# Counting eight rows of choices: one scan on VectorE and one product with ones instead of eight products

## The chip, the cores and the metric

The kernel runs on one core of a Trainium2 chip. The time is the device time of one execution in microseconds (us), as a median over several runs. The profile is of one further execution, taken by the hardware profiler. The engines are named as the profile names them: PE (TensorE, matrix products; PEld is its weight loads), DVE (VectorE), ACT (ScalarE), POOL (GpSimd), SP (SyncE, which here only issues transfers).

## The reference

A batch of 4 column-normalised attentions (over 5056 rows and 256 channels each) gives 20224 tokens of 256 channels; each token then goes to one of 8 experts, the one with the largest logit.

```python
qn = q / (norm(q, axis=1) + 1e-6);  kn = k / (norm(k, axis=1) + 1e-6)     # B, N, C = 4, 5056, 256
a = softmax(kn.T @ qn / tau)                                              # 256 x 256 for each batch
x = (v @ a).reshape(20224, 256)
logits = x @ w_gate;  e = argmax(logits)                                  # 8 experts
gate = softmax(logits)[e];  eom = sigmoid(x @ w_output_gate)[e]
out = gate * eom * (relu(x @ w1[e]) @ w2[e])                              # w1: 256 x 1024, w2: 1024 x 256
```

## The kernel before, in words

The program has three stages, which overlap.

1. `gram(b)`, one for each batch b: q and k are loaded in 20 steps of 256 rows (tiles `qk`, 6 buffers), PE adds `k.T @ q` into `s_ps` (line 467), ACT squares the same tile (line 428) and DVE adds the squares into `acc` (line 429). At the end the softmax of the 256 x 256 matrix is taken; `ah` and `al` are its high and low parts, with the attention's product with both gate matrices as 16 further columns.
2. `mix(b)`: the rows of v (tiles `v`, 4 buffers, 4 rows of each partition) are transposed on PE into `vt_ps` (line 582), split by ACT and DVE into `vh` and `vl`, and multiplied by `ah` and `al` into `x_ps` (lines 615 to 617, 272 columns: 256 of x, 8 logits, 8 output gates). ACT copies the result into `st` (line 618). A group is 128 partitions by R = 8 rows; a batch has 5 groups, the four batches 20.
3. After each group `route(b, g, st)` finds every token's expert, and a slot for it in that expert's region of the scratch `xs_d` in memory; POOL then scatters the group's 8 rows of tokens there by 8 indirect transfers (line 693). Later `blocks` fetches blocks of 256 or 128 tokens of one expert, with that expert's weights, and runs the two expert products (`h_ps`, lines 1038 to 1040; `y_ps`, lines 1063 to 1065), which take most of the time.

Stage 2 for batch b is interleaved with stage 1 for the next batches by the generator `_beside` and the rate `GRATE`. Within what the generators give, the framework's scheduler sets the order of instructions on each engine from the dependencies and its own model of durations. So a change of few instructions can move others.

In `route`, on DVE: `m` is the largest logit, `val` marks the experts that reach it, `mv` picks the first of them, and `oh` (line 656, in bfloat16, 128 x (8 rows x 8 experts)) is one where a token chose an expert. For a token in partition p and row t, its slot needs the number of earlier tokens of the group with the same choice: the tokens of the partitions above p in the same row count, and all tokens of the earlier rows (t' < t) count. PE gets this in `r_ps`, which has 9 rows of 8 columns: the product with the triangle `tri` (line 677) gives the first part, and eight products with the all-ones matrix `onesb` (line 680) add row t's total to all rows behind t; the ninth row is the total of the group. DVE then adds the running start `rco` (line 685), keeps the chosen column (line 686), sums it to the slot `si` (line 689), and moves `rco` on (line 690). The products of a group are issued one turn after its choices were found.

Of the kernel before, what the change touches and what calls it, by code (L numbers as in the profile page):

```python
# [10 lines left out]
BF16 = mybir.dt.bfloat16  # L11
F32 = mybir.dt.float32
# [3 lines left out]
ALU = mybir.AluOpType  # L16
# [4 lines left out]
P = 128  # L21
# [17 lines left out]
def tile_colnorm_attention_then_top1_moe(  # L39
# [12 lines left out]
    nc = tc.nc  # L52
    B, N, C = q.shape
    E = w_gate.shape[1]
# [6 lines left out]
    R = 8  # L61
# [32 lines left out]
    cst = ctx.enter_context(tc.tile_pool(name="cst", bufs=1))  # L94
# [4 lines left out]
    sm = ctx.enter_context(tc.tile_pool(name="sm", bufs=2))  # L99
# [49 lines left out]
    onesb = cst.tile([P, P], BF16, name="onesb")  # L149
# [3 lines left out]
        out=tri, in_=onesb, pattern=[[1, P]], compare_op=ALU.is_gt, fill=0.0, base=0, channel_multiplier=-1  # L153
# [10 lines left out]
    for b in range(B):  # L164
# [9 lines left out]
        out=real, in_=onesf[:, 0:1], pattern=[[0, 1]], compare_op=ALU.is_ge, fill=0.0, base=LASTP - 1,  # L174
# [6 lines left out]
        out=mine, in_=onesf[:, :E], pattern=[[-16, E]], compare_op=ALU.is_ge, fill=0.0, base=0, channel_multiplier=1  # L181
    )
    nc.gpsimd.affine_select(
        out=mine, in_=mine, pattern=[[16, E]], compare_op=ALU.is_ge, fill=0.0, base=15, channel_multiplier=-1
# [12 lines left out]
    nc.vector.memset(done, 0.0)  # L197
    invw = cst.tile([P, 2, E], F32, name="invw")
    nc.vector.memset(invw, 0.0)
    rank = cst.tile([P, E, E], F32, name="rank")  # L200
    rcr = cst.tile([P, E], F32, name="rcr")
    eor = cst.tile([P, E], F32, name="eor")
# [20 lines left out]
    def main(**ins):  # L223
        last.update((e, i.ins) for e, i in ins.items())

    @contextmanager
    def behind(*engines):
        with ExitStack() as held_back:
            for e in engines:
                if e in last:  # L230
                    held_back.enter_context(tc.issue_after(last[e]))
            yield
# [14 lines left out]
    def grouped(ins, group, why):  # L247
        tc.declare_no_dep(ins.ins, group=group, reason=why)
        tc.add_to_no_dep_group(group, ins.ins)
# [341 lines left out]
    def mix(b):  # L591
# [6 lines left out]
        for j in range(total):  # L598
            g, i = divmod(j, R // 2)
            n = b * total + j + AHD  # L600
            if n < B * total:
                turn(*divmod(n, total))
            if i == 0:
                if b == B - 1 and g == 1:
                    st = wide(f"st{b}_{g}")
                else:
                    st = wk.tile([P, R, CW], F32, tag="st", name=f"st{b}_{g}", bufs=STB)
                if b == B - 1 and g == 0:
                    sts["void"] = st
            vh, vl = turned.pop(0)  # L610
            for t in range(2):
                x_ps = ps_x.tile([P, 512], F32, tag="x", name="x_ps")
                for c in range(CC):
                    tsl = slice(t * P, (t + 1) * P)
                    nc.tensor.matmul(x_ps[:, :CW], vh[:, c, tsl], ah[:, c, :], start=c == 0, stop=False)  # L615
                    nc.tensor.matmul(x_ps[:, :CW], vh[:, c, tsl], al[:, c, :], start=False, stop=False)  # L616
                    ins = nc.tensor.matmul(x_ps[:, :CW], vl[:, c, tsl], ah[:, c, :], start=False, stop=c == CC - 1)  # L617
                main(PE=ins, ACT=nc.scalar.copy(st[:, 2 * i + t, :], x_ps[:, :CW]))  # L618
            if i == RLATE:
                finish(later)  # L620
            yield
            if i == R // 2 - 1:
                later = route(b, g, st)
                next(later)
# [5 lines left out]
    def route(b, g, st):  # L630
        lastg = g == NG - 1
        lg = st[:, :, C : C + E]
        og = st[:, :, C + E :]

        def t3(tag, dt=F32):
            return sm.tile([P, R, E], dt, tag=tag, name=tag)

        def t2(tag, dt=F32):
            return sm.tile([P, R], dt, tag=tag, name=tag)

        def bc(a):
            return a.unsqueeze(2).to_broadcast([P, R, E])

        def bce(a):
            return a.unsqueeze(1).to_broadcast([P, R, E])

        m = t2("r_m")
        nc.vector.tensor_reduce(out=m, in_=lg, axis=AX.X, op=ALU.max)
        d = t3("r_d")
        nc.vector.tensor_tensor(out=d, in0=lg, in1=bc(m), op=ALU.subtract)  # L650
        val = t3("r_val")
        nc.vector.scalar_tensor_tensor(out=val, in0=d, scalar=0.0, in1=bce(c8), op0=ALU.is_ge, op1=ALU.mult)
        mv = t2("r_mv")
        nc.vector.tensor_reduce(out=mv, in_=val, axis=AX.X, op=ALU.max)
        oh = t3("r_oh", BF16)
        nc.vector.tensor_tensor(out=oh, in0=val, in1=bc(mv), op=ALU.is_equal)
        if lastg and LASTP < P:
            nc.vector.tensor_scalar(out=oh, in0=oh, scalar1=real, scalar2=None, op0=ALU.mult)
        nc.scalar.activation(d, d, AF.Exp)
        se = t2("r_se")  # L660
        nc.vector.tensor_reduce(out=se, in_=d, axis=AX.X, op=ALU.add)
        nc.vector.tensor_scalar(out=se, in0=se, scalar1=1e-9, scalar2=None, op0=ALU.add)
        os_ = t3("r_os")
        nc.vector.tensor_tensor(out=os_, in0=og, in1=oh, op=ALU.mult)
        og1 = t2("r_og1")
        nc.vector.tensor_reduce(out=og1, in_=os_, axis=AX.X, op=ALU.add)
        nc.scalar.activation(og1, og1, AF.Exp, scale=-1.0)
        gt = t2("r_gt")
        nc.vector.scalar_tensor_tensor(out=gt, in0=og1, scalar=1.0, in1=se, op0=ALU.add, op1=ALU.mult)
        nc.vector.reciprocal(st[:, :, C + 1], gt)  # L670
        nc.scalar.copy(st[:, :, C].bitcast(I32), ids[:, b, g * R : (g + 1) * R])

        yield
        r_ps = ps_x.tile([P, 512], F32, tag="x", name="r_ps")
        rv = r_ps[:, : (R + 1) * E].rearrange("p (r e) -> p r e", e=E)
        with behind("PE"):
            nc.tensor.matmul(rv[:, :R, :], tri, oh, start=True, stop=False, skip_group_check=True)
            for t in range(R):
                n = R - t
                nc.tensor.matmul(  # L680
                    rv[:, t + 1 :, :], onesb, oh[:, t, :].unsqueeze(1).to_broadcast([P, n, E]),
                    start=False, stop=t == R - 1, skip_group_check=True,
                )
        rk = t3("r_rk")
        nc.vector.tensor_tensor(out=rk, in0=rv[:, :R, :], in1=bce(rco), op=ALU.add)
        nc.vector.tensor_tensor(out=rk, in0=rk, in1=oh, op=ALU.mult)
        si = sm.tile([P, R], I32, tag="r_si", name="r_si", bufs=6)
        with nc.allow_low_precision(reason="one of the terms is a whole number of a slot, the others are zero"):
            nc.vector.tensor_reduce(out=si, in_=rk, axis=AX.X, op=ALU.add)
        nc.vector.tensor_tensor(out=rco, in0=rv[:, R, :], in1=rco, op=ALU.add)  # L690
        for t in range(R):
            np_ = LASTP if lastg else P
            ins = nc.gpsimd.indirect_dma_start(  # L693
                out=xs_d[:, :],
                out_offset=bass.IndirectOffsetOnAxis(ap=si[:np_, t : t + 1], axis=0),
                in_=st[:np_, t, :].bitcast(I32),
                in_offset=None,
                bounds_check=NSLOT - 1,
                oob_is_err=False,
            )  # L700
            grouped(ins, "xs", "each token has a slot of its own; readers wait for a mark read after the scatters")
            main(POOL=ins)
# [501 lines left out]
```

## Time and profile before

| | |
|---|---|
| median of 3 runs (lowest to highest) | 1277.83 us (1277.14 to 1281.59) |
| the profiled execution: time, span | 1289.07 us, 1287.4 us |
| mean granted clock of PE, share of full speed | 0.967 |
| busy: PE, DVE, ACT, POOL | 1210.2, 705.6, 621.7, 572.3 us |
| products with `onesb` of `route` (line 680) | 160, of 64 down to 8 columns |
| products with `tri` (line 677) | 20, of 64 columns |

The busy time is the union of an engine's instructions, so overlapping ones count once. The profiled execution was 11.2 us longer than the median of the runs shown; durations below are from it.

### The profile page before, as it was taken

What the parts mean: (1) busy time and instruction counts of PE and PEld (TensorE: products, weight loads), DVE (VectorE), ACT (ScalarE), POOL (GpSimd) and SP (SyncE); (2) the same over time, 40 slices, a digit from 0 to 9 for tenths busy, and PEclk for the clock granted to TensorE, in tenths of its full rate; (3) what the DMA queues carried; (4) which work ended last, traced back from release to release, by engine and by line L of the source; (5) the groups of instructions that cost most, each with busy time, mean ns of one, the idle gap of its engine ahead of it and who ended that gap; (6) DMA issues with size and microseconds to landing.
All of it is one profiled execution on the core that took longest, in us unless ns stands there. A gap on an engine that the chain in (4) does not pass through costs nothing.

```text
span 1287.4 us, 27771 instructions
## 1 busy us (share of the span) xinstructions
PE 1210.2 (94%) x10412; PEld 1084.0 (84%) x10412; DVE 705.6 (55%) x2123; ACT 621.7 (48%) x1233; POOL 572.3 (44%) x561
## 2 busy tenths in 40 slices
PE   8999899997857999999999999999999899999998
PEld 7888788887755888888888888888888789999997
DVE  6668447544646765555565555544453355455552
ACT  5578448545542665455554555433333234344442
POOL 0004654654455224445544455544444454444443
PEclk9999899897878999999999999999999899999999
DMA  9976776754548787473646553843323633346743
GB/s 309 331 248 217 237 228 227 241 165 157 187 139 264 209 218 183 87 208 72 187 102 174 108 141 95 239 124 76 68 68 114 142 64 80 84 79 161 206 113 128
DMA packets 175170, 208.54 MB, mean 162 GB/s; under 512 B 120968, under 2 KB 124558, under 8 KB 170296
## 3 DMA queue, kind: packets, MB, share of 16 engines
q1 hardware_dynamic: 130600, 126.58, 35.1%
q0 software_dynamic: 43312, 79.73, 21.7%
q8 instruction: 84, 1.38, 0.5%
q14 instruction: 54, 0.44, 0.1%
q10 hardware_dynamic: 1120, 0.42, 0.1%
HBM read 275.55 MB, written 61.41 MB: 262 GB/s over the span
## 4 chain that ended last, share of the span: by engine, by line
PE 81%; issue 6%; DMA 4%; DVE 3%; POOL 2%; another core or an unknown queue 2%; ACT 1%; POOLq 0%; SPq 0%; DVEq 0%; ACTq 0%
PE h_ps L1040 10%; PE h_ps L1038 10%; PE h_ps L1039 10%; PE y_ps L1063 10%; PE y_ps L1065 10%; PE y_ps L1064 9%; PE s_ps L467 9%; PE x_ps L615 4%; PE x_ps L617 3%; PE x_ps L616 3%; PE vt_ps L582 3%; DMA qk<-in_k_dram 2%; POOL out_dram L1076 1%; DMA wbuf<-wsc,wi 1%
## 5 line engine op out<-in xcount | busy, mean ns | idle before, releaser
L1043 DVE SCALAR_TENSOR_TENSOR hb<-h_ps,hb 128x512 f16<-128x512 f32 (+1 forms) x360 | 226.7, 635 | 353.6 <-ACT hb L1042 265.1
L1038 PE MATMUL h_ps<-xt,wbuf 128*128 128x256 f16 (+1 forms) x1440 | 368.6, 264 | 7.3 <-DMA wbuf<-wsc,wi 4.2
L1040 PE MATMUL h_ps<-xt,wbuf 128*128 128x256 f16 (+1 forms) x1440 | 368.7, 264 | 5.2 <-issue 5.2
L1039 PE MATMUL h_ps<-xt,wbuf 128*128 128x256 f16 (+1 forms) x1440 | 368.7, 264 | 3.0 <-issue 2.8
L1065 PE MATMUL y_ps<-wbuf,hb 128*128 128x256 f16 x1296 | 354.1, 273 | 4.4 <-DVE tb_at L720 1.9
L1042 ACT ACTIVATE hb<-h_ps 128x512 f16<-128x512 f32 (+1 forms) x360 | 193.8, 550 | 340.0 <-PE h_ps L1040 238.5
L1063 PE MATMUL y_ps<-wbuf,hb 128*128 128x256 f16 x1296 | 354.5, 274 | 2.7 <-issue 2.6
L1064 PE MATMUL y_ps<-wbuf,hb 128*128 128x256 f16 x1296 | 354.4, 273 | 1.6 <-issue 1.5
L931 POOL DMA_INDIRECT wbuf<-wsc,wi x166 | 176.4, 1063 | 224.9 <-PE h_ps L1040 166.9
L693 POOL DMA_INDIRECT xs_d<-st,r_si x160 | 167.7, 1048 | 235.8 <-ACT st L618 139.4
L1076 POOL DMA_INDIRECT out_dram<-yo,b_id x162 | 171.3, 1057 | 85.7 <-issue 43.2
L1038 PEld LDWEIGHTS <-wbuf 128*128 128x128 f16 x1440 | 141.9, 99 | 22.6 <-DMA wbuf<-wsc,wi 4.5
L1040 PEld LDWEIGHTS <-wbuf 128*128 128x128 f16 x1440 | 141.9, 99 | 20.5 <-issue 6.8
L1039 PEld LDWEIGHTS <-wbuf 128*128 128x128 f16 x1440 | 141.8, 98 | 19.4 <-issue 5.5
L467 PE MATMUL s_ps<-qk 128*128 128x256 f32 x640 | 151.9, 387 | 4.4 <-DMA qk<-in_k_dram 3.9
L1065 PEld LDWEIGHTS <-hb 128*128 128x128 f16 x1296 | 127.2, 98 | 21.8 <-DVE hb L1043 2.5
L1063 PEld LDWEIGHTS <-hb 128*128 128x128 f16 x1296 | 127.2, 98 | 19.6 <-issue 5.2
L1064 PEld LDWEIGHTS <-hb 128*128 128x128 f16 x1296 | 127.3, 98 | 16.6 <-issue 2.5
L467 PEld LDWEIGHTS s_ps<-qk 128*128 128x128 f32 x640 | 120.1, 194 | 19.7 <-DMA qk<-in_k_dram 3.9
L615 PE MATMUL x_ps<-ah,vh 128*128 128x272 f32 x320 | 108.0, 340 | 27.3 <-ACT st L618 13.7
L947 POOL DMA_INDIRECT xg<-xs_d,gi x49 | 50.8, 1037 | 156.3 <-DVE xr L1013 141.8
L429 DVE TENSOR_TENSOR acc<-acc,sq 128x1024 f32<-128x1024 f32 x76 | 92.9, 1223 | 43.6 <-ACT sq L428 26.7
(196 smaller groups left out, 1514.4 us busy)
## 6 DMA issues: line engine op xcount, KB each, us to landing
qk<-in_q_dram SPq DMA_DIRECT2D x75, 256.0 KB
qk<-in_k_dram SPq DMA_DIRECT2D x75, 256.0 KB
v<-in_v_dram SPq DMA_DIRECT2D x32, 512.0 KB
raw<-in_moe_w_dram SPq DMA_DIRECT2D x14, 1024.0 KB
xg<-xs_d SPq DMA_DIRECT2D x30, 272.0 KB
wsc<-whi SPq DMA_DIRECT2D x14, 512.0 KB
wsc<-wlo SPq DMA_DIRECT2D x14, 512.0 KB
v<-in_v_dram SPq DMA_DIRECT2D x8, 480.0 KB
```

Source lines behind the costliest of these rows:

```text
L467: nc.tensor.matmul(s_ps[:, c, :], kt[:, 1, t, c * P : (c + 1) * P], qt[:, 0, t, :], start=st == 0 and t0 == 0 and t == 0 and c == 0 and n ...
L693: ins = nc.gpsimd.indirect_dma_start(out=xs_d[:, :], out_offset=bass.IndirectOffsetOnAxis(ap=si[:np_, t : t + 1], axis=0), in_=st[:np_, t, ...
L931: nc.gpsimd.indirect_dma_start(out=wbuf[half][:, at_of(u), :], out_offset=None, in_=wsc[half][:end, :], in_offset=bass.IndirectOffsetOnAxi ...
L1038: nc.tensor.matmul(hp, w1s[:, 0, c, fs], xh, start=fi == 0 and c == 0, stop=False, **KWM)
L1039: nc.tensor.matmul(hp, w1s[:, 0, c, fs], xl, start=False, stop=False, **KWM)
L1040: main(PE=nc.tensor.matmul(hp, w1s[:, 1, c, fs], xh, start=False, stop=fin, **KWM))
L1042: main(ACT=nc.scalar.activation(hh, h_ps[:, :, :w], AF.Relu))
L1043: ins = nc.vector.scalar_tensor_tensor(out=hb[:, 1, 2 * fp : 2 * fp + 2, :w], in0=h_ps[:, :, :w], scalar=0.0, in1=hh, op0=ALU.max, op1=ALU ...
L1063: nc.tensor.matmul(y_ps[:, t, :], hb[:, 0, f, tsl], w2s[:, 0, f, :], start=st, stop=False, **KWM)
L1064: nc.tensor.matmul(y_ps[:, t, :], hb[:, 0, f, tsl], w2s[:, 1, f, :], start=False, stop=False, **KWM)
L1065: main(PE=nc.tensor.matmul(y_ps[:, t, :], hb[:, 1, f, tsl], w2s[:, 0, f, :], start=False, stop=fin, **KWM))
L1076: ins = nc.gpsimd.indirect_dma_start(out=out[:, :], out_offset=bass.IndirectOffsetOnAxis(ap=un["id"][:, t : t + 1], axis=0), in_=un["yo"][ ...
```

## The change

`route` now writes `oh` so that the 8 rows of one expert lie side by side (a tile of 128 x (8 experts x 8 rows), read through a view as rows by experts). A scan on DVE runs along these 64 values: state = `again` * state + choice, where the constant `again` is 0 at each expert's first row and 1 elsewhere, so that `upto` holds, for each row t, the number of choices of that expert in rows 0 to t of the partition. One product of `onesb` with `upto`, 64 columns, is added to rows 1 to 8 of `r_ps`, in the place of the eight. The constant `again` is made at the start by two memsets.

```diff
+    again = cst.tile([P, E * R], F32, name="again")
+    nc.vector.memset(again, 1.0)
+    nc.vector.memset(again.rearrange("p (e r) -> p e r", r=R)[:, :, 0:1], 0.0)
...
-        oh = t3("r_oh", BF16)
+        flat = sm.tile([P, E * R], BF16, tag="r_oh", name="r_oh")
+        oh = flat.rearrange("p (e r) -> p r e", r=R)
         nc.vector.tensor_tensor(out=oh, in0=val, in1=bc(mv), op=ALU.is_equal)
         if lastg and LASTP < P:
             nc.vector.tensor_scalar(out=oh, in0=oh, scalar1=real, scalar2=None, op0=ALU.mult)
+        upto = sm.tile([P, E * R], BF16, tag="r_up", name="r_up")
+        nc.vector.tensor_tensor_scan(
+            out=upto, data0=again, data1=flat, initial=0.0, op0=ALU.mult, op1=ALU.add
+        )
+        upto = upto.rearrange("p (e r) -> p r e", r=R)
...
             nc.tensor.matmul(rv[:, :R, :], tri, oh, start=True, stop=False, skip_group_check=True)
-            for t in range(R):
-                n = R - t
-                nc.tensor.matmul(
-                    rv[:, t + 1 :, :], onesb, oh[:, t, :].unsqueeze(1).to_broadcast([P, n, E]),
-                    start=False, stop=t == R - 1, skip_group_check=True,
-                )
+            nc.tensor.matmul(rv[:, 1:, :], onesb, upto, start=False, stop=True, skip_group_check=True)
```

Lines of `route` behind the scan move down by 9 and those behind the products by 4, and all lines between the new constant and `route` by 3.

The PE's order at the first group, before: the products of `r_ps` stand between two triples of `x_ps` (six of the eight products with ones are left out at the end of this piece).

```order
L677 LDWEIGHTS tri
L677 MATMUL r_ps<-r_oh,tri 128x64
L680 LDWEIGHTS onesb
L680 MATMUL r_ps<-r_oh,onesb 128x64
L680 LDWEIGHTS onesb
L680 MATMUL r_ps<-r_oh,onesb 128x56
```

The same place now:

```order
L686 LDWEIGHTS tri
L686 MATMUL r_ps<-r_oh,tri 128x64
L687 LDWEIGHTS onesb
L687 MATMUL r_ps<-r_up,onesb 128x64
L618 MATMUL x_ps<-ah_550,vh 128x272
```

Seven products with their weight loads are gone from each of the 20 groups; the triple of `x_ps` follows directly.

DVE's order at the first group, before (numbers behind a name tell tiles of one name apart):

```order
L654 TENSOR_REDUCE r_mv<-r_val 128x8
L661 TENSOR_REDUCE r_se<-r_d 128x8
L656 TENSOR_TENSOR r_oh<-r_val,r_mv 128x64
L662 TENSOR_SCALAR r_se<-r_se 128x8
L664 TENSOR_TENSOR r_os<-st_0_598,r_oh 128x64
L666 TENSOR_REDUCE r_og_758<-r_os 128x8
```

And now, where the scan is the row that writes `r_up`:

```order
L657 TENSOR_REDUCE r_mv<-r_val 128x8
L670 TENSOR_REDUCE r_se<-r_d 128x8
L660 TENSOR_TENSOR r_oh<-r_val,r_mv 128x8x8
L671 TENSOR_SCALAR r_se<-r_se 128x8
L664 SCALAR_TENSOR_TENSOR r_up<-again,r_oh 128x64
L673 TENSOR_TENSOR r_os<-st_0_601,r_oh 128x64
L675 TENSOR_REDUCE r_og_763<-r_os 128x8
```

The scan stands between the choices and the rest of the group's gate.

SP's queue in the part where the third batch's q and k (`qk_9` to `qk_15` are steps 9 to 15 of its gram) and the second batch's v (`v_1_0` is the first half of its second group) are loaded, before:

```order
L444 DMA qk_12_1783<-in_q_dram 128x512
L444 DMA qk_12_1783<-in_k_dram 128x512
L576 DMA v_1_0_1721<-in_v_dram 128x1024
L444 DMA qk_13_1793<-in_q_dram 128x512
L444 DMA qk_13_1793<-in_k_dram 128x512
L576 DMA v_1_2_1826<-in_v_dram 128x1024
```

And now:

```order
L447 DMA qk_12_1761<-in_q_dram 128x512
L447 DMA qk_12_1761<-in_k_dram 128x512
L447 DMA qk_13_1771<-in_q_dram 128x512
L447 DMA qk_13_1771<-in_k_dram 128x512
L447 DMA qk_14_1834<-in_q_dram 128x512
L447 DMA qk_14_1834<-in_k_dram 128x512
L447 DMA qk_15_1869<-in_q_dram 128x512
L447 DMA qk_15_1869<-in_k_dram 128x512
L579 DMA v_1_0_1699<-in_v_dram 128x1024
```

Six loads of the third batch's gram now stand ahead of `v_1_0`. On PE the same batch's gram moves ahead with them. Counted in PE's order at the product with `tri`, 49.75 of the 80 gram steps stood ahead of the fourth group and 53.75 stand there now; at the seventh group it is 60.75 and 60.25, at the twelfth 78 and 78, and from the thirteenth on all 80 are done in both. POOL's order is the same in both.

## The prediction

> **What bounds the kernel now.** I read the page's busy times and its chain first, then the busy times by stage, then the lines of `route` and the waits around it.
>
> ```profile
> span 1287.4 us, 27771 instructions
> PE 1210.2 (94%) x10412; PEld 1084.0 (84%) x10412; DVE 705.6 (55%) x2123; ACT 621.7 (48%) x1233; POOL 572.3 (44%) x561
> PE 81%; issue 6%; DMA 4%; DVE 3%; POOL 2%; another core or an unknown queue 2%; ACT 1%; POOLq 0%; SPq 0%; DVEq 0%; ACTq 0%
> ```
>
> The reader is to see that PE is the bound on average: it is busy for 94% of the span and is 81% of the chain that ends last. The change touches only `route`, and its products fall into two of the stages below (columns: PE, PEld, DVE, ACT, POOL busy, granted clock, DMA share, GB/s).
>
> ```profile
> 96.00:291.00 195.00, 180.70 (x1225) 166.06 (x1224) 113.58 (x307) 109.99 (x239) 102.41 (x96) 0.96 0.67 219
> 291.00:425.00 134.00, 98.87 (x677) 87.54 (x677) 75.07 (x326) 63.52 (x153) 70.66 (x69) 0.78 0.59 194
> 425.00:1270.00 845.00, 827.96 (x7915) 739.16 (x7913) 450.65 (x1379) 382.55 (x748) 391.32 (x371) 1.00 0.52 130
> ```
>
> From 96 to 291 us `mix` runs beside the grams of later batches, and PE is busy 180.7 of 195 us (93%). From 291 to 425 us, when the grams are done, it is busy 98.9 of 134 us (74%) at a clock of 0.78: there PE is not the bound. From 425 us the expert products fill it to 98%; no instruction of the change is there. How the 20 groups lie in the first two stages:
>
> ```profile
> L680 PE MATMUL r_ps<-r_oh,onesb 128*128 128x64 bf16 (+7 forms) x160 | 7.4, 183 | 0.0
> L680 PE MATMUL r_ps<-r_oh,onesb 128*128 128x64 bf16 (+3 forms) x96 | 4.2, 179 | 0.0
> ```
>
> The first row is for the whole span, the second for the window from 96 to 291 us: 96 of 160 products, so 12 groups lie where PE is the bound and 8 where it is not.
>
> **The change part by part.** *The removed products.* The first group in time order:
>
> ```profile
> 96.05 0.28 PE L615 MATMUL x_ps<-ah,vh 128*128 128x272 f32 x1
> 96.17 0.29 PE L616 MATMUL x_ps<-al,vh 128*128 128x272 f32 x1
> 96.30 0.28 PE L617 MATMUL x_ps<-ah,vl 128*128 128x272 f32 x1
> 96.42 0.10 PEld L677 LDWEIGHTS <-tri 128*128 128x128 bf16 x1
> 96.44 0.28 PEld L680 LDWEIGHTS <-onesb 128*128 128x128 bf16 x8
> 96.46 0.35 PE L680 MATMUL r_ps<-r_oh,onesb 128*128 128x64 bf16 x8
> 96.65 0.19 PEld L615 LDWEIGHTS x_ps<-ah,vh 128*128 128x128 f32 x1
> ```
>
> A product's duration (183 ns in the mean) is not what it costs: eight of them together last 0.35 us, because they overlap. What they keep PE from is the time from the first weight load of line 680 to the next weight load of other work, 96.65 - 96.44 = 0.21 us for eight, 0.026 us each. Seven fewer save 7 x 0.026 = 0.18 us in a group. In the 12 groups of the PE-bound stage that is 12 x 0.18 = 2.2 us, on the path. In one group at a low clock the same distance is larger:
>
> ```profile
> 295.92 0.43 PEld L680 LDWEIGHTS <-onesb 128*128 128x128 bf16 x8
> 296.27 0.29 PEld L582 LDWEIGHTS vt_ps<-ident,v 128*128 128x128 f32 x2
> ```
>
> Here it is 0.35 us, so seven cost 0.31 us. For the 8 groups behind 291 us the saving is between 8 x 0.18 and 8 x 0.31, 1.4 to 2.5 us of PE's time; I count nothing, because PE idles 35 us of that stage, and the waits there are on other things:
>
> ```profile
> DVE r_rk L685 <- remote: 12.0, 3, 5.2
> DVE vl L588 <- ACT vh L586: 11.9, 6, 6.3
> PE x_ps L615 <- ACT st L618: 11.8, 7, 4.6
> ```
>
> These are waits of the window from 290 us on. `r_rk`, the reader of the products, is held three times for 12.0 us in all by something the profile does not name, not by the products. If that cover were gone, the 8 groups would give up to 2.5 us more.
>
> *The two products that stay.* They now read their 64 columns at a distance of 8 elements. No row shows a read of that kind. Their price is between that of a product of line 680, 0.026 us, and that of a product of 272 columns in the rows above, 96.30 - 96.17 = 0.13 us. The upper end is 2 x 0.10 x 12 = 2.5 us and would take the gain away. I take the lower, since type and number of columns are the same.
>
> *The scan.* No row has one of 64 elements. The nearest:
>
> ```profile
> L762 DVE TENSOR_TENSOR_SCAN tb_cx<-onesf,tb_n 128x8 f32<-128x8 f32 x3 | 0.5, 165 | 0.0
> L768 DVE SCALAR_TENSOR_TENSOR tb_r<-tb_cx,tb_r 128x8 f32<-128x8 f32 x3 | 0.5, 162 | 0.0
> L652 DVE SCALAR_TENSOR_TENSOR r_val<-r_d,c 128x64 f32<-128x64 f32 x20 | 4.5, 224 | 0.5
> ```
>
> For 8 elements a scan costs what another operation of two inputs costs. For 64 the other operation takes 224 ns; 56 more elements are 62 ns, 1.1 ns each. So the scan is at least 224 ns, and if each element cost twice, 224 + 64 x 1.1 = 294 ns. I take 260 ns, in the middle: 20 x 0.26 = 5.2 us of DVE. [...]
>
> DVE is busy 113.6 of 195 us in the PE-bound stage, so its 12 scans (3.1 us) lie in its idle time. Whether PE must wait for the scan is a matter of distance:
>
> ```profile
> L656 DVE TENSOR_TENSOR r_oh<-r_val,r_mv x20: 211/222/294, 91.0 to 396.5; 128x64 bf16<-128x64 f32 x20
> L677 PE MATMUL r_ps<-r_oh,tri x20: 193/203/277, 96.4 to 397.2; 128*128 128x64 bf16 x20
> ```
>
> In the first group the choices begin at 91.0 us and PE takes them at 96.4 us, 5.4 us later: the scan fits. In the last group the distance is only 0.7 us, and 0.26 us of scan may show. Behind the scan in DVE's queue are `r_os` and the gate's sums, then a `vl` that PE needs, later by a quarter of a microsecond. In the 8 groups behind 291 us that is at most 8 x 0.29 = 2.3 us on the path, and at least nothing; I count nothing, as their PE saving. The rows of `r_oh` (writing with a distance between elements now) keep their 224 ns: the range of that row, 211 to 294 ns, bounds it to 20 x 0.07 = 1.4 us of DVE, likewise hidden. The two memsets of 64 elements run while DVE waits for POOL's number rows at the start.
>
> *The moved work.* The third batch's gram is up to 4 steps ahead of where it was, and six loads stand ahead of a v load on SP. A load of v that comes late would hold PE's transposes (line 582), then `vh` and `vl`. In the new order the gram products that free the six `qk` buffers stand well ahead of that v's transposes, and DMA is 67% busy in that stage, so I count nothing; PE's total is the same, and both orders agree from the twelfth group on.
>
> *Sum.* 1289.07 - 2.2 = 1286.9 us for the profiled execution. That one is 11.2 us above the median of the runs, so against the median it is 1277.8 - 2.2 = 1275.6, in round numbers 1276 us.
>
> **The rivals.** All within 0.5% (6.4 us, about what a measurement of this kernel can tell from no change) is *A*, the forecast. *B*, the change gives nothing: the 2.2 us come back as the scan's 2.3 us in the last 8 groups, or as the slower strided reads; 1277.9 us. For it: the choices of the last group are only 0.7 us ahead of PE. Against it: the waits above.
>
> *C*, slower: the gram of the third batch is used up earlier, PE runs out of filling work between the groups, and its clock falls. The clock is either full or half:
>
> ```profile
> 161.60:165.00 3.40, 3.40 (x16) 3.12 (x15) 2.98 (x8) 1.55 (x4) 1.48 (x2) 0.50 0.91 303
> 229.90:236.70 6.80, 6.15 (x21) 5.29 (x22) 4.48 (x14) 4.23 (x11) 2.38 (x3) 0.50 0.68 233
> 383.50:390.30 6.80, 4.42 (x20) 3.87 (x21) 3.19 (x13) 3.09 (x7) 3.02 (x3) 0.50 0.18 64
> ```
>
> A half-clock stretch of 6.8 us costs up to 3.4 us of PE's work where PE is the bound. Three more of them in the stage before 291 us are 10.2 us, less 2.2: 1285.8 us. It decides from the third on, (6.4 + 2.2) / 3.4 = 2.5. For it: the stage already has such stretches (its clock is 0.96, 4% of 195 us = 7.8 us lost). Against it: the orders meet again by the seventh group, with 20 gram steps left in both. [...]
>
> *D*, faster: the new order closes waits. PE idles 195 - 180.7 = 14.3 us of that stage; a third of that and of the 7.8 us, 7.4 us, with the 2.2 us, give 1268.2 us. For it: gram products can fill any wait for `x_ps`. Against it: nothing in the change aims there.
>
> **How the numbers follow.** A 0.58, B 0.12, C 0.15, D 0.15. A and B are within 0.5%: 0.70; D is faster, C slower. The predicted time is A's, 1276 us. The range goes to D's 1268 and C's 1286 with a microsecond below for the 2.5 us that the last 8 groups may give: 1267 to 1286 us.
>
> **What would show it.** Right: `r_ps` with 40 products instead of 180, the distance from the weight load with `tri` to the next `x_ps` or gram load down from 0.23 to about 0.05 us; 20 scans of 224 to 294 ns; PE's busy time from 425 us on unchanged. Wrong: a clock below 0.94 or PE busy less than 177 us in the stage before 291 us (C), or that stage shorter by over 5 us (D); waits of PE for the scan; in the last 8 groups a longer distance from `r_oh` to `r_si`.

## The result, and the profile after

On the chip on which both were timed the changed kernel took 1289.8 us in the median, the kernel before 1280.6 us: ratio 1.0066, 95% interval 1.0041 to 1.0091. It is slower by 0.66%. The forecast was 1276 us and no measurable change; slower had a chance of 0.15.

The profiled execution took 1293.51 us. Its page, its stages (same columns as before) and the lines of `route`:

```profile
span 1291.8 us, 27524 instructions
PE 1206.9 (93%) x10272; PEld 1076.1 (83%) x10272; DVE 712.6 (55%) x2145; ACT 619.2 (48%) x1233; POOL 568.5 (44%) x561
...
96.00:291.00 195.00, 175.98 (x1074) 157.91 (x1073) 115.08 (x305) 104.95 (x230) 94.06 (x88) 0.91 0.64 210
291.00:425.00 134.00, 93.91 (x625) 82.05 (x624) 70.34 (x298) 61.55 (x152) 66.36 (x67) 0.81 0.51 169
425.00:1270.00 845.00, 829.96 (x7937) 740.88 (x7935) 458.71 (x1427) 385.95 (x756) 398.97 (x381) 1.00 0.53 135
...
L660 DVE TENSOR_TENSOR r_oh<-r_val,r_mv 128x64 bf16<-128x64 f32 x20 | 8.8, 441 | 0.3
L664 DVE TENSOR_TENSOR_SCAN r_up<-again,r_oh 128x64 bf16<-128x64 f32 x20 | 5.8, 289 | 0.4
L690 DVE TENSOR_TENSOR r_rk<-r_rk,r_oh 128x64 f32<-128x64 f32 x20 | 5.3, 266 | 0.3
L673 DVE TENSOR_TENSOR r_os<-st,r_oh 128x64 f32<-128x64 f32 x20 | 5.0, 248 | 0.0
L686 PE MATMUL r_ps<-r_oh,tri x20: 267/272/313, 96.2 to 415.0; 128*128 128x64 bf16 x20
```

Three of these rows as they were before (lines 656, 686 and 664 there):

```profile
L656 DVE TENSOR_TENSOR r_oh<-r_val,r_mv 128x64 bf16<-128x64 f32 x20 | 4.5, 224 | 0.3
L686 DVE TENSOR_TENSOR r_rk<-r_rk,r_oh 128x64 f32<-128x64 f32 x20 | 4.4, 222 | 0.4
L664 DVE TENSOR_TENSOR r_os<-st,r_oh 128x64 f32<-128x64 f32 x20 | 4.4, 220 | 0.0
```

PE has 140 products fewer and is busy 3.3 us less, and yet the span is longer. In the stage from 96 to 291 us PE got through 1074 products instead of 1225, busy 176.0 us instead of 180.7, at a clock of 0.91 instead of 0.96. Of these 151 products, 84 are those that the change takes out of the 12 groups there; 67 are work that was not reached in time. From 291 to 425 us it is 52 fewer, of which the change takes out 56. The last group's product with `tri` comes at 415.0 us instead of 397.2. Behind 425 us nothing more is lost: of the 17.8 us by which the last group is late, 4.4 us are left at the end of the span (1291.8 against 1287.4 us). The write of `r_oh` went from 224 to 441 ns and the scan takes 289 ns.

A part of the lost time is of an unusual kind. Two stretches of the changed kernel, same columns:

```profile
371.00:379.00 8.00, 0.00 (x0) 0.00 (x0) 0.08 (x1) 0.00 (x0) 5.85 (x6) 0.63 0.52 180
403.00:409.00 6.00, 0.00 (x0) 0.00 (x0) 0.00 (x0) 0.01 (x1) 2.84 (x3) 0.50 0.76 212
```

For 8 us, and again for 6 us, PE, DVE and ACT do almost nothing, while POOL issues scatters one by one. What ACT and PE waited for at the end of the first one:

```profile
368.19 0.60 PE L585 MATMUL vt_ps<-ident,v 128*128 128x128 f32 x4
...
377.67 0.97 POOL L697 DMA_INDIRECT xs_d<-st,r_si  x1 [0.30 <-issue]
379.18 0.59 ACT L589 CAST vh<-vt_ps 128x512 fp32r<-128x512 f32 x1 [9.40 <-remote]
...
380.10 0.59 PE L618 MATMUL x_ps<-ah,vh 128*128 128x272 f32 x1 [9.45 <-ACT vh L589]
```

The transposes that ACT needs were done by 368.8 us; ACT began 10.4 us later, half a microsecond after the last scatter of the group was issued. I call such a stretch a standstill: over 2 us, between 96 and 430 us, in which no instruction (weight loads included) begins on PE, DVE or ACT. The trace of before has 10.8 us of them, this one 25.6 us.

### The profile page after: what moved, and what is told of

The parts are those of the page before. It is cut to its first block, busy times and chain, and to the rows that moved or that the text cites. A ratio compares the mean times of both kernels' runs of the same rounds, so it can differ in the third digit from the quotient of the medians.

```text
span 1291.8 us, 27524 instructions
## 1 busy us (share of the span) xinstructions
PE 1206.9 (93%) x10272; PEld 1076.1 (83%) x10272; DVE 712.6 (55%) x2145; ACT 619.2 (48%) x1233; POOL 568.5 (44%) x561
## 4 chain that ended last, share of the span: by engine, by line
PE 62%; issue 4%; DMA 2%; another core or an unknown queue 2%; ACT 2%; DVE 2%; POOL 1%; POOLq 0%; SPq 0%; ACTq 0%; DVEq 0%
PE h_ps L1044 10%; PE h_ps L1042 10%; PE h_ps L1043 10%; PE y_ps L1069 10%; PE y_ps L1067 10%; PE y_ps L1068 10%; DMA wbuf<-wsc,wi 1%; DMA xt<-xr 1%; POOL out_dram L1080 1%; PE x_ps L618 0%; POOL wbuf L935 0%; PE x_ps L620 0%; ACT st L621 0%; PE x_ps L619 0%
## 5 line engine op out<-in xcount | busy, mean ns | idle before, releaser
L470 PE MATMUL s_ps<-qk 128*128 128x256 f32 x640 | 156.7, 395 | 7.7 <-DMA qk<-in_q_dram 3.9
L470 PEld LDWEIGHTS s_ps<-qk 128*128 128x128 f32 x640 | 123.2, 199 | 27.0 <-issue 7.8
L618 PE MATMUL x_ps<-ah,vh 128*128 128x272 f32 x320 | 105.1, 332 | 27.2 <-ACT vh L589 9.4
L1016 ACT ACTIVATE xr<-xg,b_sx 128x256 f16<-128x256 f32 x162 | 74.2, 501 | 89.1 <-DVE b_sx L259 57.5
```

Of the source, the lines that this page charges most:

```text
L470: nc.tensor.matmul(s_ps[:, c, :], kt[:, 1, t, c * P : (c + 1) * P], qt[:, 0, t, :], start=st == 0 and t0 == 0 and t == 0 and c == 0 and n ...
```

## The experiments

There were seven chips in all, counted in the order of the sets (the first may be the same chip as a later one), and they are of two kinds. The kernel before takes 1281 us on the first, fourth and seventh (medians 1280.6, 1281.2, 1280.9) and 1200 us on the second, third, fifth and sixth (1201.4, 1199.1, 1199.7, 1199.6). Each ratio below is to before on the same chip.

### The changed kernel on other chips

Three runs of the unchanged text of after.

> The kernel after once more, on this chip beside the others: both theories 1.0066, within 0.004.

> The kernel after once more. On the first chip (before 1280.6 us) it was 0.66% slower, on the second (before 1201.4 us) 0.45% faster. Freezes: the two chips differ in stretches in which no engine but POOL moves while POOL issues a group's eight scatters (four of about 5 to 9 us in the slower trace of after, none on the second chip); where before is near 1280 and such stretches are in the trace, after is at 1.006, where before is near 1201 it is at 0.9955, each within 0.004. Chance of the chip alone: the ratio has no relation to the time of before.

> The kernel after, as the anchor of this set. Near 1281 us for before: 1.0066 within 0.003. Near 1200: 0.995 within 0.003. All the theories agree on it.

Measured: 0.9955 (0.9936 to 0.9973) on the second chip, 0.9949 (0.9928 to 0.9971) on the third, 0.9938 (0.9917 to 0.9959) on the fifth: 1193 to 1195 us. On chips of the 1200 kind the change makes the kernel faster by half a per cent; the first expectation was wrong, with both of its theories. Page and stages of the run on the fifth chip:

```profile
span 1191.4 us, 27524 instructions
PE 1168.7 (98%) x10272; PEld 1060.2 (89%) x10272; DVE 720.7 (60%) x2145; ACT 623.5 (52%) x1233; POOL 563.3 (47%) x561
...
96.00:291.00 195.00, 192.93 (x1343) 182.34 (x1342) 140.23 (x405) 131.22 (x296) 117.97 (x112) 1.00 0.75 247
291.00:425.00 134.00, 125.68 (x1103) 113.28 (x1102) 104.61 (x390) 86.44 (x179) 75.50 (x75) 1.00 0.90 262
371.00:379.00 8.00, 7.37 (x68) 6.36 (x65) 3.51 (x12) 4.32 (x10) 3.44 (x5) 1.00 1.13 333
```

It is the same program, with PE busy 192.9 of 195 us where it was 176.0, and with no standstill (the 13 traces from chips of this kind have 0 to 3.7 us of them). So the two kinds ask different questions: on the 1200 kind PE is busy 94 to 99% of these two stages (98% of the span), on the 1281 kind it waits between the groups (busy 90% and 70% of the two in the first trace of after).

### Before once more, for a trace of it

> The kernel before itself, for a trace of it on the chip of this set. Ratio 1.000. If the time is near 1200 as on the second and third chip: no stretch in which only POOL moves, under 20 us of half clock (87 us in its trace on the first chip), and of the runs of the changed kernels that lasted longer than after there, it shares the wait of an expert's product for its weights near 745 us (2.7 us, with 3.4 us at half clock behind it), which the two traces of after on those chips do not have.

This one fell on the fourth chip: 1.0004 (0.9965 to 1.0042). Its trace has the same two stages as the first trace of before, with 8.0 us of standstills:

```profile
96.00:291.00 195.00, 178.71 (x1206) 162.28 (x1203) 114.45 (x307) 108.61 (x238) 101.55 (x95) 0.96 0.68 216
291.00:425.00 134.00, 97.45 (x684) 87.63 (x683) 74.46 (x326) 63.26 (x154) 72.68 (x71) 0.80 0.59 193
...
L677 PE MATMUL r_ps<-r_oh,tri x20: 189/203/277, 95.7 to 399.9; 128*128 128x64 bf16 x20
```

The low numbers of the changed kernel in the stage from 96 us are thus not due to an odd trace of before. What before would show on a chip of the 1200 kind was not seen in a trace of its own; the kernels with its order stand in for it below.

### The order alone

The rate at which gram steps are handed to the scheduler, in before and in after. In before no instruction is added or removed; ahead of the second to sixth group's product with `tri` stand 45.5, 48.75, 50.25, 54 and 59 gram steps in PE's order, instead of 45, 47.5, 49.75, 53.75 and 56.25 (after has 46.25, 50.5, 53.75, 57 and 59.5). The first two of the expectations below pair these numbers with the group before the right one: up to the sixth group the shift is 0.25 to 2.75 steps. Behind it the new rate also moves work: ahead of the eleventh group stand 77 steps instead of 72 (after 73.5), ahead of the twelfth 80 instead of 78 (after 78). So this is another reordering of like size, largest at the eleventh group with 5 steps, and not the change's own, which is largest at the fourth with 4.

```diff
-    GRATE = 1.3
+    GRATE = 1.35
```

> The kernel before with the rate by which the scheduler hands out gram steps raised from 1.3 to 1.35: no instruction is added or removed, but ahead of the second, third and fourth group's tri product stand 48.75, 50.25 and 54 gram steps (before 45, 47.5, 49.75; after 46.25, 50.5, 53.75). Order: slower than before, by 0.4 to 0.9%, with more time at half clock between 96 and 291 us. VectorE: same as before, 1.000 within 0.003.

> The kernel before at the rate of 1.35 once more: no instruction added or removed, the gram's third batch pulled ahead to 48.75, 50.25, 54 and 59 steps at the groups 2 to 5 (after at the same rate: 49.5, 51, 55 and 59, measured at 1.0072 where before took 1281 us). Near 1281 us for before: 1.005 to 1.009 if the order makes the loss, at most 1.002 if the instructions of the change do. Near 1200: 1.000 within 0.002, as on the second chip.

> The kernel after with the scheduler's rate of gram steps at 1.35 instead of 1.3: the same instructions, ahead of the third and fourth group's tri product 49.5 and 51 gram steps (after 50.5 and 53.75, before 47.5 and 49.75). If the order of the gram in batch three decides: between after and the held kernel, on the second and third chip (after 0.995, held 1.002) 0.997 to 1.002, on a chip like the first below after's 1.0066. If the instructions decide: as after, 0.995 or 1.0066.

Measured: before's instructions in this order, 0.9998 (0.9979 to 1.0017) on the second chip, and 1.0064 (1.0027 to 1.0101) on the seventh, of the 1281 kind. After's instructions in nearly the same order, 1.0072 (1.0046 to 1.0098) on the fourth, of the same kind. The rows of the latter two, before's instructions first:

```profile
96.00:291.00 195.00, 179.66 (x1231) 163.94 (x1230) 116.03 (x311) 111.12 (x242) 99.24 (x92) 0.97 0.68 218
291.00:425.00 134.00, 93.78 (x669) 82.25 (x668) 70.17 (x301) 60.01 (x149) 72.81 (x72) 0.83 0.57 186
L677 PE MATMUL r_ps<-r_oh,tri x20: 189/202/213, 97.1 to 403.5; 128*128 128x64 bf16 x20
```

```profile
96.00:291.00 195.00, 176.00 (x1109) 160.49 (x1107) 115.90 (x302) 108.86 (x234) 96.82 (x88) 0.95 0.65 211
291.00:425.00 134.00, 95.53 (x631) 85.17 (x631) 76.61 (x324) 60.81 (x152) 71.88 (x71) 0.80 0.55 179
L686 PE MATMUL r_ps<-r_oh,tri x20: 268/272/320, 98.2 to 411.1; 128*128 128x64 bf16 x20
```

Before at 1.35 on the seventh chip is the run that says most. On a chip of the 1281 kind a reordering alone, with no instruction of the change, costs 0.64%, as much as the change (between the means over all its 12 runs and all 17 of before the difference is 0.52%). What the change's instructions add in that order is 1.0072 less 1.0064, 0.1%, from two chips, with the two intervals leaving about 0.45% to either side. On the 1200 kind the same order costs nothing. That the change's own reordering costs as much is inferred from this: no run on a chip of the 1281 kind has the change's order without its instructions, or its instructions in the order of before.

How an order is paid for shows less clearly. In both runs the groups come later (last `tri` at 403.5 and 411.1 us against 397.2 and 399.9 in the two traces of before) and there are more standstills (17.3 and 23.6 us against 10.8 and 8.0), but the clock of the first stage is 0.97 and 0.95, not 0.91: its fall belongs to that one trace of after. Measured at equal work (PE's products other than those of `r_ps`), the way from the first group to the seventh takes 106.2 us in after and 107.4 in after at 1.35, but 98.8 and 100.6 us in the traces of before and 100.8 us in before at 1.35. From the twelfth group to the last it is 125.7 and 125.1 us, against 118.1 and 118.9, and 123.6 us in before at 1.35. So the later part of the delay is there with the reordering alone, and the earlier part only in the two traces with the change's instructions. These are single executions; that of before at 1.35 took 1286 us, near those of before, so its rows show less than its median of 1288.7 us says. That a reordering alone can cost this much is shown; by which waits, and how much of the change's own loss is its order, is not settled.

### The gram held back in the changed kernel

One product of the third batch's gram (step 8) may not pass the work emitted before it. Ahead of the third to sixth group's `tri` then stand 48, 48, 51.75 and 56 gram steps, up to 2 fewer than in before (the 51.75 of the first expectation is the fifth group's, not the fourth's).

```diff
-                            nc.tensor.matmul(
+                            with behind(*(('PE',) if b == 2 and st == 8 and t == 0 and c == 0 else ())):
+                                nc.tensor.matmul(
```

> The kernel after, with one product of the third batch's gram (step 8) held behind the product emitted last before it, so that the gram isn't pulled ahead: ahead of the fourth group's tri product stand 51.75 gram steps where after has 53.75 and before 49.75, ahead of the third 48 (50.5 and 47.5). VectorE's work is that of after. Order: ratio to before at most 1.002. VectorE: 1.006 as after, within 0.003.

> The kernel after with step 8 of the third batch's gram held, so that fewer gram steps are pulled ahead of the groups 2 to 4, once more (1.0015 on the chip at 1201 us, where after was 0.9955). If before is near 1280 here: by the order theory at most 1.002, by the VectorE theory 1.006. If before is near 1201: 1.0015 within 0.002, that is, the order of the gram alone moves the time by 0.6%, as much as the whole change.

> The kernel after with step 8 of the third batch's gram held. If the order of the gram makes the loss on chips like the first: at most 1.003 there, 0.004 or more below after of this set. If it is the instructions: as after of this set within 0.003. Near 1200 us for before: 1.002 as twice before.

> The kernel after with step 8 of the third batch's gram held. Near 1281 us for before: if the gram's order makes the loss, at most 1.003; if VectorE's work does, 1.005 to 1.009. Near 1200: 1.002 to 1.004 as three times before.

Measured: 1.0015 (0.9998 to 1.0033), 1.0024 (1.0008 to 1.0041), 1.0035 (1.0019 to 1.0052) and 1.0027 (1.0005 to 1.0049) on the second, third, fifth and sixth chip, all of the 1200 kind; what it does on the other kind is open. Here it says something else: with the same instructions as after, in another order of some grams, the gain of 0.5% is gone and a loss of 0.2 to 0.3% is in its place. One of the places, 720 to 780 us on the third chip, after first, held second, with the wait that makes the difference:

```profile
720.00:780.00 60.00, 59.42 (x547) 53.08 (x544) 35.47 (x107) 27.43 (x54) 29.50 (x28) 1.00 0.69 187
```

```profile
720.00:780.00 60.00, 57.29 (x511) 50.58 (x510) 33.55 (x95) 26.59 (x53) 29.55 (x28) 0.97 0.70 182
...
PE y_ps L1068 <- DMA wbuf<-wsc,wi: 2.7, 1, 2.7
```

An expert's product waits 2.7 us for its weights, and 3.4 us of half clock follow. Of the 13 traces of the 1200 kind all but the three of after have this wait (1.7 to 3.0 us of idle PE in that stretch, against 0.3 to 0.6 in after), those with before's order too. Nothing of the change is within 300 us of it. For the same work around this wait (some 90 us of products) the traces of after take 3.0 us less in the mean than those of the held kernel, whose spans are 7.3 us longer, and 2.7 us less than the four of dve_same, dead_strided, dve_dead4 and before at 1.35, whose products are those of before. So about half of the 5 to 7 us gained on these chips is an order in which one late wait happens not to occur; the price of the products, below, has about 2 us of the rest.

### VectorE's work alone

Four kernels add work on DVE in each group and leave its result unused; TensorE's products and, but for half a gram step, the order are those of before (with four scans it shifts by up to 1.25 steps).

```diff
 # dve_dead: two of these ahead of the write of r_oh; dve_dead4: four
+nc.vector.tensor_tensor_scan(out=upto, data0=again, data1=val.rearrange("p r e -> p (r e)"), initial=0.0, op0=ALU.mult, op1=ALU.add)
 # dead_strided: one write in the new layout; dve_same: this, and a scan of flat behind r_oh
+nc.vector.tensor_tensor(out=flat.rearrange("p (e r) -> p r e", r=R), in0=val, in1=bc(mv), op=ALU.is_equal)
```

> The kernel before with two more scans of 64 elements ahead of the write of r_oh in each group, their results unused: 0.58 us more of VectorE on each group's chain, as much as the change adds there, with r_oh as it was and TensorE's instructions and (but for a quarter of a gram step) their order unchanged. If VectorE's added time is on the path: +0.6% (up to 20 times 0.58 us is 11.6 us). If it lies beside other work: 1.000 within 0.003.

> The kernel before with one more write of the same choices in the change's layout, 441 ns of VectorE ahead of the write of r_oh in each group, its result unused; all else and the order as before. If VectorE's time as such is on the path: three quarters of dve_dead's 0.33%, 1.0025 on a chip like the first. If the strided write hurts beyond its own time (others' accesses wait for it): 1.005 or more. Where before is near 1200: 1.000 within 0.003 if TensorE has other work meanwhile.

> The kernel before with four unused scans ahead of the write of r_oh instead of two: 1.16 us of VectorE per group, 23 us in all (the gram's order shifts by up to 1.5 steps in five places). If VectorE's chain is on the path on chips like the first: twice dve_dead, 1.006 to 1.009. If dve_dead's 1.0033 was chance of the runs: 1.000 to 1.002. Where before is near 1200: 1.000 within 0.003 if it lies beside other work.

> The kernel before with the strided write and the scan of the change added beside r_oh, their result unused: 0.73 us of VectorE per group (441 + 289 ns), where the change adds 0.58; TensorE's products read r_oh as before, and the order is that of before but for a quarter or half of a gram step. Near 1281 us for before: if VectorE's work makes the loss, 1.006 to 1.010; if the order or TensorE's side makes it, at most 1.004. Near 1200: 1.000 within 0.003.

Measured: dve_dead 1.0033 (1.0005 to 1.0061) on the fourth chip, of the 1281 kind; dead_strided 1.0001 (0.9978 to 1.0025) and dve_dead4 1.0037 (1.0016 to 1.0058) on the fifth and dve_same 0.9991 (0.9973 to 1.0009) on the sixth, of the 1200 kind. The rows that dve_same adds take as long as those of the change:

```profile
L659 DVE TENSOR_TENSOR r_fl<-r_val,r_mv 128x64 bf16<-128x64 f32 x20 | 8.8, 442 | 0.3
L664 DVE TENSOR_TENSOR_SCAN r_fl<-again,r_fl 128x64 bf16<-128x64 f32 x20 | 5.7, 287 | 0.0
```

On the 1200 kind this much of DVE's time, 0.73 us a group, is hidden; 1.16 us a group is not wholly, or its shifted order costs. On the 1281 kind 0.55 us a group (281 and 267 ns) costs between 0.05 and 0.61%: a part of the change's loss may be DVE's, from next to nothing to nearly all, and this run alone does not say. That a reordering alone gives 0.64% makes a large part for DVE less likely, but does not exclude it.

### The products

dve_part is after with the eight products kept; pe_more2 is before with 14 further products in each group, of `onesb` by a tile of zeros.

```diff
 # dve_part, against after
-            nc.tensor.matmul(rv[:, 1:, :], onesb, upto, start=False, stop=True, skip_group_check=True)
+            for t in range(R): ...                 # the eight products of before, reading oh in its new layout
 # pe_more2, against before: twice
+            for t in range(R - 1):
+                nc.tensor.matmul(rv[:, t + 1 :, :], onesb, none[:, t, :].unsqueeze(1).to_broadcast([P, R - t, E]), start=False, stop=False, skip_group_check=True)
```

> The kernel before with the new layout of r_oh and the scan, while its eight products stay (the scan's result is left unused); TensorE's instructions stand as before. Two theories of the +0.66%. Order: the scheduler's new order, which calls up the third batch's gram earlier, costs the time; then this run equals before, ratio 1.000 within 0.003, and its stretch 96 to 291 us has the clock near 0.95. VectorE: the strided write (441 against 224 ns) and the scan (289 ns) lengthen each group's chain by some 0.5 us, 20 groups, about 10 us; then this run is at 1.006 to 1.009, with the clock of that stretch near 0.91.

> The kernel before with the new layout and the scan, eight products kept, once more (1.0016 on the chip at 1201 us). If before is near 1280 here: by the order theory 1.000 within 0.003, by the VectorE theory 1.006 to 1.010. If before is near 1201: 1.0016 within 0.002, and the products alone are then worth what after lies below it, 5 to 7 us.

> The kernel before with 14 more products of the ones matrix by zeros in each group, of the shapes of the seven that the change removes, twice over; the sum in r_ps stays what it was. By the prediction's price (0.026 us each, all of it on the path while TensorE is never idle) 14 x 0.026 x 20 is 7.3 us, ratio 1.006; by the prediction's reasoning on the first chip (12 groups count) 4.4 us, 1.0034. If the products' time doesn't reach the end at all: 1.000 within 0.002.

Measured: dve_part 1.0016 (0.9997 to 1.0034) on the second chip and 1.0020 (1.0001 to 1.0039) on the third. It did not tell the theories apart, and it wasn't the clean half of the change that I took it for: its eight products read the new layout, and that costs them. The first group there, then in dve_same, where the products read the old layout, then in after on the fifth chip:

```profile
97.57 0.10 PEld L686 LDWEIGHTS <-tri 128*128 128x128 bf16 x1
97.58 0.68 PEld L689 LDWEIGHTS <-onesb 128*128 128x128 bf16 x8
98.19 0.19 PEld L618 LDWEIGHTS x_ps<-ah,vh 128*128 128x128 f32 x1
```

```profile
96.99 0.10 PEld L685 LDWEIGHTS <-tri 128*128 128x128 bf16 x1
97.00 0.29 PEld L688 LDWEIGHTS <-onesb 128*128 128x128 bf16 x8
97.22 0.19 PEld L618 LDWEIGHTS x_ps<-ah,vh 128*128 128x128 f32 x1
```

```profile
99.10 0.10 PEld L686 LDWEIGHTS <-tri 128*128 128x128 bf16 x1
99.12 0.10 PEld L687 LDWEIGHTS <-onesb 128*128 128x128 bf16 x1
99.20 0.21 PEld L618 LDWEIGHTS x_ps<-ah,vh 128*128 128x128 f32 x1
```

From the load of `tri` to the next other load: 0.62, 0.23 and 0.10 us (medians over the 20 groups 0.63, 0.23 and 0.10). Nine reads at a distance cost 0.39 us more than nine in the old layout, 0.043 us each. pe_more2 took 1.0082 (1.0056 to 1.0107) on the fourth chip: 280 products cost 10.5 us (7.2 to 13.7), 0.038 us each, where the prediction had 0.026 in 12 groups and nothing in eight. That is no clean price: its order is shifted by up to 1.25 gram steps, and on this kind of chip a reordering can cost 0.64% by itself.

## Why the prediction was wrong

*The moved work* is the step that failed: a term put at nothing. The prediction saw that the third batch's gram moves ahead, asked for late loads of v and for idle PE, and wrote "so I count nothing". On the kind of chip that was forecast a reordering of like size, with no instruction changed, was worth 0.64%, 8.2 us, almost four times the gain that was summed up. How much of the change's own loss is its order stays open, because the second term put at nothing, DVE's added work, may have a part there (dve_dead: 0.05 to 0.61%).

Rival C named the moved gram, and its number was near: 1285.8 us was 0.62% above the median shown then; measured were 0.66%. Its two signs, a clock below 0.94 and PE busy less than 177 us, are both in the trace of after (0.91, 175.98). That the clock is either full or half holds in the traces of before and after, whose records of the granted clock are all 1.0 or 0.5. That it falls because PE runs out of work was C's assumption: the stages of before show the two side by side (clock 0.96 with PE busy 93%, 0.78 with 74%, 1.00 with 98%), not which comes of which. But C's account of the payment, three half-clock stretches, is borne out by that trace alone (34 us at half clock in the stage, against 17 us in before); after at 1.35 had a clock of 0.95 there and before at 1.35 one of 0.97, so that its number came so near is in part luck. The argument against it, that both orders meet again with 20 gram steps left, did not hold: at the seventh group, where nearly the same work is done in both, `tri` comes at 202.3 us in the trace of after and at 195.9 and 197.0 us in those of before, and the lag grows up to the last group (415.0 against 397.2 and 399.9).

*The removed products.* Right in sign, too large. By the prediction's own distance a group saves 0.23 - 0.10 = 0.13 us, not 0.18, because the two remaining products read at a distance of 8 elements. Their bounds were 0.026 and 0.13 us each; I took the lower for having the same type and columns, and they cost about 0.05 (0.10 us for the two). On the 1200 kind, where PE is busy 98% of the span, 20 groups give 20 x 0.13 = 2.6 us. The span less PE's idle time and less half of its half-clock time is 1165.0 us in the mean of after's three traces there, and 1167.2 us in the four of dve_same, dead_strided, dve_dead4 and before at 1.35: 2.2 us, which agrees. The four held kernels, with after's products, have 1164.8 us. What the removed products are worth on the 1281 kind no run shows.

*The write of `r_oh`.* It kept its 224 ns in the sum, with 294 as the bound; it is 441 ns. The row gave bounds for a write of neighbouring elements, and this one isn't: its neighbours are 8 elements apart. Other traces with this layout have 440 to 446 ns for the row, on both kinds of chip (441 in after at 1.35 on the fourth, 440 and 443 in the held kernel and in after on the fifth, 446 in dve_part on the third); those with the old one on the fourth and the seventh have 210 to 224 ns (dve_dead, before, before at 1.35, pe_more2). In dve_same the write in the old layout, right behind one in the new, takes 352 ns. The products' reads at this distance cost too, 0.043 us more each. Why, no run shows: beside neighbouring elements only the step of 8 was tried.

*The scan.* 289 ns within the 224 to 294 given, where 260 was taken. Other traces that hold it behind `r_oh` have 288 to 294 ns (288 in after at 1.35, after on the fifth chip and dve_part on the third, 294 in the held kernel on the fifth). That is the upper end, the estimate in which each element costs twice. The scans of 8 elements in before took 165 ns, so 56 more are 124 ns, 2.2 ns each, where the row beside them had 1.1; the middle was too low.

*DVE in all.* Per group 217 ns for the write, 289 for the scan, 28 and 44 ns for the two readers of `r_oh` (`r_os` 248 against 220, `r_rk` 266 against 222 ns), 0.58 us, 11.6 us over the kernel where the prediction had 5.2. That it is hidden holds on the 1200 kind (dve_same); on the other kind dve_dead leaves it open.

*The base.* The sum started from 1277.8 us, the median of three runs; 22 runs gave 1280.6. That is 2.8 of the 13.8 us between forecast and result.

*The chances.* What the prediction called the likeliest, a small gain from products, was present and was worth 2 us. Beside it stood a term that it could not price from the trace, the reordering: another order was worth 8 us on one kind of chip, and the held kernel's order against after's, same instructions, 7 to 12 us on the other. Such a term deserved the wider range and more than 0.15.

No kernel of these beats both everywhere: after is the fastest on the 1200 kind (1193 to 1195 us), before on the 1281 kind.

## What to carry to other kernels

When a scheduler sets the order, price the reordering by itself: change a number that moves only the order, as the rate of the grams did here, and see how far the time goes; an instruction's saving that is smaller than this spread can't be told from it. The price of a new access pattern isn't bounded by a row that reads or writes neighbouring elements (here 441 ns, where that row had 211 to 294). And ask, before reading a stage as bound by an engine, whether it is so on every chip: the same stage, 96 to 291 us, kept PE busy 90 to 93% on one kind and 97 to 100% on the other.

## What the runs showed of the hardware

Chips differ by almost 7% in this kernel, 1281 against 1200 us, and it isn't the speed of instructions: the median distance between two products of `h_ps` from 450 to 1150 us is 109 ns on both, between two of the gram from 96 to 330 us 216 ns on both. What differs is pauses, and time at half clock: 65 to 93 us of the span in the traces of the 1281 kind, 1 to 17 us in the others. From 450 to 1150 us the traces of the 1281 kind have 13 to 23 distances of over 0.5 us between products, 10.7 to 21.0 us in all, those of the 1200 kind 1 to 4; between 96 and 430 us the former have 8 to 26 us of standstills, the latter 0 to 3.7. The five longest (5.2 to 8.3 us) lie where POOL issues the scatters of the groups; some end with the last scatter, others before or after it. Why the engines stand still there, and only on some chips, no run tells: no kernel with fewer or other scatters was tried.
